# Other row lengths for the first query and key loads, turning by products with the identity, and held gelus spread over slots

## The chip, the cores and the metric

The kernel runs on one core of one Trainium2 chip. The core has TensorE (PE; its weight loads are listed as PEld), VectorE (DVE), ScalarE (ACT), GpSimd (POOL) and SyncE (SP); DMAs are issued from queues on SP, ACT and POOL and share 16 DMA engines. Matmuls write to PSUM banks, from which DVE or ACT copy the result. The metric is the device time of one execution in microseconds (us). The kernel before was run 8 times: median 1395.11 us (1392.54 to 1398.53).

## What is computed

```python
scores = scale * np.matmul(q, k.transpose(0, 1, 3, 2))          # q, k, v: (8, 8, 576, 64) fp32
thresh = np.max(scores, axis=-1, keepdims=True) - tau
scores = np.where(scores >= thresh, scores, -1000000000.0)
attn = softmax(scores)                                          # sum + 1e-9 below the line
x = attn @ v -> (4608, 512)
h = x @ w_in; g = gelu(h); out = g @ w_out                      # w_in 512x2048, w_out 2048x512
```

The weights w_in and w_out are float64 in memory. The kernel converts them to float32 on the chip.

## The kernel before

**Attention by pairs and slots.** Two heads make a pair p, 32 pairs in all, four of them (0 to 3) belonging to the first batch and called early. The 576 rows of a pair's queries are cut into four chunks of 128 and a tail of 64; one (pair, chunk) is a slot. The main loop (L823) runs over slots in an order written out by hand: slots 0 to 7 are chunks 0 and 1 of pairs 0 to 3, slots 8 to 19 are chunks 2, 3 and 4 of pairs 0 to 3, and from slot 20 (BATCH) on each pair has five slots in a row. All engines execute what the loop emits in the order in which it emits it, each engine its own part.

**One slot.** `scores` (PE, L348) multiplies a chunk of qT with kT into a "sc" tile. `softmax_head` takes the negated maximum (DVE, L360), a threshold (POOL, L361) and the exponential (ACT, L363). `weigh_v` (PE, L465, for chunks that came due) multiplies the turned p with v into a tile xT, which ACT copies into `x_blk` (L470). `softmax_tail` applies the threshold and sums (DVE, L379, L382). For early pairs `diagonal` (DVE L390, ACT L393) makes a diagonal matrix of the reciprocals, and in the next slot `turn_p_early` turns p by products with that diagonal (PE, L291); ACT copies the turned p out of PSUM (L299, L302, L309, L314). Later pairs are turned by DVE (`turn_p`, L426) and DMAs.

**Queries and keys of the early pairs.** `load_early` brings the rows of a pair's two heads side by side into a tile of 128 columns per chunk. q has row c*128+p on partition p, in pieces of 256 bytes; k has row 4p+c, read as 1 KB in one run and written in pieces of 256 bytes. SP issues them, but for k of pairs 0 (ACT) and 1 (POOL). `turn_qk_early` transposes each chunk on PE (L265, tails L273) and ACT copies the result into qT, kT and q_tail (L268 to L278). It runs for pair 0 ahead of the loop and for pair p+1 in the slot of pair p and chunk 0 (slots 0, 2, 4).

**The conversion of the weights.** 32 pieces (128x512 float64, two DMAs each, `load_piece`) are converted in steps by DVE with one step on ACT (`conversions`, L168 to L178, nominal 340, 340, 720 and 700 ns on DVE). Two pieces are loaded ahead of the loop, one in slot 0, one in slot 2, and then each finished piece calls for the next one. `convert(ns)` in each slot adds a budget and does steps until it is used up: 0 in slot 0, 3400 in slots 1 to 7, 3650 in slots 8 to 18, and everything left in slot 19.

**The MLP between slots.** `block_steps` multiplies a block of 256 tokens: 16 chunks of hidden units with four products each (L536), two chunks to a PSUM tile hT, then gelu on ACT, then layer 2 (L550) into a tile o. `fill` emits as many of these products in each slot as a goal written by hand allows; for slots 10 to 19 that is 0.42 of block 0. The gelu and the exponential use different ACT tables, so `gelus` only copies hT to SBUF (L503) while `hold` is set and puts it on a list `held`; the other finished hT wait on a list `late`. At slot 20 `gelus_held` applies the gelu to all held tiles (L509), and `table` (L522) brings the exponential's table back.

**PSUM.** The pool `ps` has four one-bank buffers with the tag "mm": the tiles tr, xT, hT and o all come from it. The scores have the tag "sc" and their own buffers.

After slot 20 the remaining blocks go on beside attention; the last ten blocks are computed by `strassen` (L670), which the diff doesn't touch.

Of the kernel before, what the change touches and what calls it, by code (L numbers as in the profile page):

```python
# [8 lines left out]
FP32 = mybir.dt.float32  # L9
# [9 lines left out]
def kernel(  # L19
# [28 lines left out]
    nc = tc.nc  # L48
    ctx.enter_context(tc.manual_schedule())

    B, H, S, D = q.shape
    d_model, d_ff = moe_w_in.shape
    P = 128
    Q = 32
    HP = H // 2
    NP = B * HP
    EARLY = HP
    NC = S // P
    MAIN = NC * P
    TAIL = S - MAIN  # L60
# [4 lines left out]
    N_DF = d_ff // P  # L65
    TOK = 256
# [119 lines left out]
    def convert(ns):  # L186

        if conv["steps"] is None:
            conv["steps"] = conversions()
        conv["debt"] += ns  # L190
        while conv["debt"] > 0:
            took = next(conv["steps"], None)
            if took is None:
                return
            conv["debt"] -= took
# [3 lines left out]
    x_blk = {}  # L199
# [27 lines left out]
    def load_early(p):  # L227
        b, hp = divmod(p, HP)
        s = st[p] = {}
        for name, src in (("q", q), ("k", k)):  # L230
            t = s[name] = ld.tile([P, NC + 1, P], FP32, tag=name, name=name)
            eng = (nc.scalar, nc.gpsimd)[p] if p < 2 and name == "k" else nc.sync
            for e in range(2):
                order = "(t p) d -> p t d" if name == "q" else "(p t) d -> p t d"
                eng.dma_start(
                    t[:, 0:NC, e * D:(e + 1) * D], src[b, 2 * hp + e, 0:MAIN, :].rearrange(order, p=P))
            eng.dma_start(
                t[0:TAIL, NC, :].rearrange("p (e d) -> p e d", e=2),
                src[b, 2 * hp:2 * hp + 2, MAIN:S, :].rearrange("e s d -> s e d"),
            )  # L240

    def load_v_early(p):
        b, hp = divmod(p, HP)
# [5 lines left out]
    def turn_qk_early(p):  # L249


        s = st[p]
        if 2 <= p < HP:
            qT = op.tile([P, MAIN], FP32, tag="o_sb", name="qT")
            kT = pd_tail[p - 2].rearrange("p b i -> p (b i)")
        else:
            qT = ld.tile([P, MAIN], FP32, tag="qT", name="qT")
            kT = ld.tile([P, TAIL + S], FP32, tag="kT", name="kT")
        s["qT"], s["kT"] = qT, kT
        qt = s["q_tail"] = q_tail[p % 4]  # L260
        for name in "qk":
            t = s[name]
            tr = ps.tile([P, NC, P], FP32, tag="mm", name="tr")
            for c in range(NC):
                nc.tensor.transpose(tr[:, c, :], t[:, c, :], ident)  # L265
            src = tr.rearrange("p c s -> p (c s)")
            if name == "q":
                nc.scalar.activation(qT, src, AF.Copy, bias=0.0, scale=q_scale)  # L268
            else:
                nc.scalar.copy(kT[:, TAIL:S], src)  # L270
        tr = ps.tile([P, NC, P], FP32, tag="mm", name="tr")
        for j, name in enumerate("qk"):
            nc.tensor.transpose(tr[:, j, 0:TAIL], s.pop(name)[0:TAIL, NC, :], ident[0:TAIL, 0:TAIL])  # L273
        nc.scalar.copy(kT[:, S:S + TAIL], tr[:, 1, 0:TAIL])
        nc.scalar.copy(kT[D:P, 0:TAIL], tr[D:P, 1, 0:TAIL])
        for e in range(2):
            rows = slice(e * D, (e + 1) * D)
            nc.scalar.activation(  # L278
                qt[rows, e * TAIL:(e + 1) * TAIL], tr[rows, 0, 0:TAIL], AF.Copy, bias=0.0, scale=q_scale[rows])

    def turn_p_early(p, i):


        s = st[p]
        if i == 0 or (p < HP and i == 2):
            s["pT"] = [one.tile([P, KR, S], FP32, tag=f"pT{e}", name=f"pT{e}") for e in range(2)]
        w, diag = s.pop(("p", i)), s.pop(("diag", i))
        n = 1 if i == NC else 2

        def turn(to, cols, e):  # L290
            nc.tensor.matmul(to, lhsT=w[:, cols], rhs=diag[:, e, :], start=True, stop=True)  # L291

        for e in range(n):
            tr = ps.tile([P, NC, P], FP32, tag="mm", name="tr")
            for c in range(NC):
                at = e * (S + TAIL) + c * P
                turn(tr[:, c, :], slice(at, at + P), e)
            if i < NC:
                nc.scalar.copy(s["pT"][e][:, 0:NC, i * P:(i + 1) * P], tr)  # L299
        if i == NC:  # L300
            for e in range(2):
                nc.scalar.copy(s["pT"][e][:, 0:NC, MAIN:S], tr[:, :, e * TAIL:(e + 1) * TAIL])  # L302
        tails = s["pT"][0][:, NC, :]
        tr = ps.tile([P, NC, P], FP32, tag="mm", name="tr")
        if i < NC:
            for e in range(2):
                at = MAIN + e * TAIL
                turn(tr[e * TAIL:(e + 1) * TAIL, 0, :], slice(at, at + TAIL), e)
            nc.scalar.copy(tails[:, i * P:(i + 1) * P], tr[:, 0, :])  # L309
            return  # L310
        turn(tr[0:TAIL, 0, :], slice(MAIN, S), 0)
        for e in range(2):
            rows = slice(e * TAIL, (e + 1) * TAIL)
            nc.scalar.copy(tails[rows, MAIN:S], tr[0:TAIL, 0, rows])  # L314

    def scale_q(p):
        t = st[p]["q"]
# [132 lines left out]
    def weigh_v(p, lo, hi):  # L450


        b, hp = divmod(p, HP)
        s = st[p]
        xT = ps.tile([P, 512], FP32, tag="mm", name="xT")
        for c in range(KR):
            for e in range(2):
                f = slice(e * D, (e + 1) * D)
                to = xT[f, 0:hi - lo]
                if p < EARLY:  # L460
                    rhs = s["pT"][0 if c == NC else e][:, c, lo:hi]
                else:
                    to = to.rearrange("p (g s) -> p g s", s=2 * Q)
                    rhs = by_64(s["pT"][e])[:, lo // (2 * Q):hi // (2 * Q), c, :]
                nc.tensor.matmul(  # L465
                    to, lhsT=s["v"][:, e, c, :], rhs=rhs, start=(c == 0), stop=(c == KR - 1))
        for n, o, at, size in in_blocks(b, lo, hi):
            if n not in x_blk:
                x_blk[n] = xg.tile([P, N_DM, TOK], FP32, tag="x", name="x")
            nc.scalar.copy(x_blk[n][:, hp, o:o + size], xT[:, at - lo:at - lo + size])  # L470

    def in_blocks(b, lo, hi):
        while lo < hi:
# [22 lines left out]
    def gelus(left):  # L496


        while len(late) > left:
            g, j, hT = late.pop(0)  # L500
            t = gp.tile([P, 2, TOK], FP32, tag="g", name="g")
            if hold[0]:
                nc.scalar.copy(t, hT)  # L503
                held.append((g, j, t))
            else:
                gelu(g, j, t, hT)
# [3 lines left out]
        g[j - 1], g[j] = t[:, 0, :], t[:, 1, :]  # L510
        dirty[0] = True

    def gelus_held():
        hold[0] = False
        while held:
            g, j, t = held.pop(0)
            gelu(g, j, t, t)

# [6 lines left out]
    def block_steps(n):  # L525

        g = {}
        mlp["layer"] = 1
        for j in range(N_DF):
            if j % 2 == 0:  # L530
                hT = None
            for c in range(N_DM):
                yield NS_IN, (j * P // PIECE + 1) * N_DM
                if hT is None:
                    hT = ps.tile([P, 2, TOK], FP32, tag="mm", name="hT")
                nc.tensor.matmul(hT[:, j % 2, :], lhsT=w_in_sb[c][:, j * P:(j + 1) * P], rhs=x_blk[n][:, c, :],  # L536
                                 start=(c == 0), stop=(c == N_DM - 1))
            if j % 2:
                late.append((g, j, hT))
                gelus(lag[0])  # L540
        for m in range(TOK // P):
            for j in range(N_DF):
                mlp["layer"] = 2
                yield NS_OUT, len(pieces) - N_DF + j + 1
                if j not in g:
                    gelus(0)
                    gelus_held()
                if j == 0:
                    o = ps.tile([P, 512], FP32, tag="mm", name="o_ps")
                nc.tensor.matmul(o[:, 0:d_model], lhsT=g[j][:, m * P:(m + 1) * P], rhs=w_out_sb[j],  # L550
                                 start=(j == 0), stop=(j == N_DF - 1))
            o_sb = op.tile([P, d_model], FP32, tag="o_sb", name="o_sb")
            nc.scalar.copy(o_sb, o[:, 0:d_model])
            row = n * TOK + m * P
            nc.sync.dma_start(out[row:row + P, :], o_sb)
# [267 lines left out]
    for n in range(len(slots) + WEIGH + 1):  # L823
# [5 lines left out]
            softmax_head(p, i)  # L829
        elif n == len(slots):  # L830
            ext = weights_in()
        gelus(0)
        if n == BATCH:
            gelus_held()
        table()
        for args in due:
            weigh_v(*args)
# [46 lines left out]
            scale_q(p + 1)  # L884
        if p >= HP - 1 and i == 2 and p + 1 < NP:
            turn_qk(p + 1)
        convert(0 if n == 0 else 3400 if n < 2 * HP else 3650 if n < BATCH - 1 else 1e9)
        if early:
            diagonal(p, i)
        if not early:  # L890
# [51 lines left out]
```

## Time and profile before

| what | value |
|---|---|
| median of 8 runs | 1395.11 us (1392.54 to 1398.53) |
| the profiled execution | 1392.52 us, span 1390.7 us |
| PE busy | 1359.2 us, 98% |
| DVE busy | 891.4 us, 64% |
| ACT busy | 640.9 us, 46% |
| POOL busy | 432.3 us, 31% |
| mean granted TensorE clock | 0.994 |
| DMA queue q1 (SP and others) | 194768 packets, 112.84 MB |
| DMA queue q0 (POOL) | 23488 packets, 54.77 MB |

The profile is of one execution. The span runs from the first instruction to the last; 1.8 us of the execution's time lie around it. "Busy" counts the time in which an engine had an instruction running, whatever bounds it. Views that are used below: the busy share in 40 slices of the span, in tenths; the chain of work that ended last; tables of busy time by stretches of time, with the granted clock (1.00 is full speed) and the DMA engines' mean share; and timelines, in which each row is a start, a duration, an engine, a line, an operation, what it writes and reads, its count, and in brackets how long the engine had stood idle and what released it. A product in fp32 has two records on PE, a transpose one.

### The profile page before, as it was taken

The page shows a single profiled execution, that of the slowest core. Times are in us where ns is not written, and L with a number is a line of the kernel's source. Part 1 is how long each engine was busy: PE and PEld are TensorE (multiplying, and loading weights), DVE is VectorE, ACT ScalarE, POOL GpSimd, SP SyncE. Part 2 cuts the span into 40 slices and gives each one's busy share as a digit, 9 for nine tenths or more (in the row PEclk, how much of TensorE's full clock was granted, in tenths as well). Part 3 has the DMA queues.
Part 4 walks back from the last instruction along what each step waited for, and adds up shares of the span by engine and source line. Part 5 has one row for each costly group of instructions (what it writes and reads, how often), then busy time and mean ns, then how long its engine had stood idle before and what let it go on. Part 6 is the DMA issues. An engine that isn't in the chain of part 4 may idle for free.

```text
span 1390.7 us, 19980 instructions
## 1 busy us (share of the span) xinstructions
PE 1359.2 (98%) x6608; PEld 967.7 (70%) x6608; DVE 891.4 (64%) x1734; ACT 640.9 (46%) x1165; POOL 432.3 (31%) x895
## 2 busy tenths in 40 slices
PE   6799899999999999999999999999999999999999
PEld 5676557557457466466466475588888888888887
DVE  5889677788888888888888888764132232241330
ACT  6666636547547457448367357241141240330420
POOL 4444254455455555554554551100000000000000
PEclk9899999999999999999999999999999999999999
DMA  9989267667777777787788776500000001001000
GB/s 264 270 296 292 56 135 166 131 158 169 168 163 177 160 187 183 156 195 178 157 201 180 158 181 132 118 0 8 23 1 23 23 1 46 16 0 53 9 8 23
DMA packets 219557, 169.18 MB, mean 122 GB/s; under 512 B 121456, under 2 KB 203952, under 8 KB 219456
## 3 DMA queue, kind: packets, MB, share of 16 engines
q1 hardware_dynamic: 194768, 112.84, 36.1%
q0 software_dynamic: 23488, 54.77, 13.3%
q8 instruction: 54, 0.88, 0.3%
q10 hardware_dynamic: 1200, 0.30, 0.1%
q14 instruction: 47, 0.39, 0.1%
HBM read 72.73 MB, written 12.52 MB: 61 GB/s over the span
## 4 chain that ended last, share of the span: by engine, by line
PE 89%; DVE 5%; ACT 3%; DMA 2%; issue 1%; SPq 1%; POOL 0%; DVEq 0%; ACTq 0%; POOLq 0%
PE bank L670 35%; PE o_ps L550 16%; PE hT L536 14%; PE sc L348 12%; PE xT L465 10%; DVE p L379 1%; ACT p L363 1%; PE tr L291 1%; DVE power L176 1%; DMA raw<-in_moe_w_out_dram 1%; ACT diag L393 1%; DVE power L168 1%; DVE w_in L178 0%; DVE nmx L360 0%; DVE w_out L178 0%
## 5 line engine op out<-in xcount | busy, mean ns | idle before, releaser
L363 ACT ACTIVATE p<-sc,nmx 128x576 f32<-128x576 f32 x288 | 201.9, 738 | 270.3 <-DVE nmx L360 270.2
L379 DVE SCALAR_TENSOR_TENSOR p<-sc,thr,p 128x576 f32<-128x576 f32 x288 | 225.4, 816 | 70.4 <-ACT p L363 67.6
L360 DVE TENSOR_REDUCE nmx<-sc 128x1 f32<-128x576 f32 x288 | 205.3, 750 | 67.4 <-PE sc L348 66.6
L536 PE MATMUL hT<-x,w_in 128*128 128x256 f32 x1024 | 241.1, 385 | 0.0
L550 PE MATMUL o_ps<-w_out,g 128*128 128x512 f32 x512 | 236.8, 603 | 2.1 <-ACT pT L302 2.1
L536 PEld LDWEIGHTS hT<-x,w_in 128*128 128x128 f32 x1024 | 189.5, 190 | 49.2 <-issue 23.5
L361 POOL TENSOR_SCALAR thr<-nmx,tau_eff 128x1 f32<-128x1 f32 x288 | 84.0, 292 | 394.5 <-DVE nmx L360 394.1
L550 PEld LDWEIGHTS o_ps<-w_out,g 128*128 128x128 f32 x512 | 92.9, 189 | 112.7 <-issue 108.6
L465 PE MATMUL xT<-pT,v 128*64 128x256 f32 (+1 forms) x1280 | 163.9, 409 | 0.5 <-issue 0.5
L348 PE MATMUL sc<-kT,qT 64*128 64x288 f32 x960 | 158.6, 433 | 3.3 <-DVE p L379 1.7
L426 DVE STREAM_TRANSPOSE turned_p<-p 128x1152 f32<-128x1152 f32 x112 | 154.4, 1378 | 3.9
L348 PEld LDWEIGHTS sc<-kT,qT 64*128 64x128 f32 x960 | 90.6, 188 | 76.8 <-issue 64.4
L465 PEld LDWEIGHTS xT<-pT,v 128*64 128x64 f32 x1280 | 89.0, 137 | 72.9 <-issue 13.3
L670 PE MATMUL bank<-x,w_in 128*128 128x256 f32 x480 | 116.7, 379 | 0.0
L670 PE MATMUL bank<-w_out,unit 128*128 128x256 f32 x520 | 115.5, 379 | 0.0
L223 POOL DMA_DIRECT2D v<-in_v_dram x208 | 110.7, 535 | 4.7 <-issue 3.1
L670 PEld LDWEIGHTS bank<-w_out,unit 128*128 128x128 f32 x520 | 98.8, 190 | 13.4
L670 PEld LDWEIGHTS bank<-x,w_in 128*128 128x128 f32 x480 | 91.2, 190 | 12.8 <-issue 0.5
L670 PE MATMUL bank<-v,unit 128*128 128x256 f32 x320 | 82.1, 379 | 0.0
L214 POOL DMA_DIRECT2D q<-in_q_dram x104 | 70.7, 685 | 10.0 <-issue 9.1
L670 PE MATMUL bank<-unit,turned_p 128*128 128x256 f32 x320 | 73.1, 379 | 0.0
L522 ACT ACT_TABLE_LOAD x56 | 71.8, 1283 | 1.0
(154 smaller groups left out, 1486.7 us busy)
## 6 DMA issues: line engine op xcount, KB each, us to landing
pT<-turned_p SPq DMA_DIRECT2D x448, 160.0 KB, 3.7
pT<-pd_tail SPq DMA_DIRECT2D x112, 80.0 KB, 3.1
q<-in_q_dram POOLq DMA_DIRECT2D x104, 72.0 KB, 3.3
k<-in_k_dram POOLq DMA_DIRECT2D x104, 72.0 KB, 3.2
inv<-turned SPq DMA_DIRECT2D x56, 128.0 KB, 4.0
v<-in_v_dram POOLq DMA_DIRECT2D x156, 40.0 KB, 3.2
x<-x SPq DMA_DIRECT2D x10, 512.0 KB, 4.6
raw<-in_moe_w_out_dram POOLq DMA_DIRECT2D x8, 512.0 KB, 5.5
```

Of the source, the lines that this page charges most:

```text
L223: eng.dma_start(t[r:P:4, e, 0:n, :], rows[:, r * KR:r * KR + n, :])
L348: nc.tensor.matmul(sc[e][:, h, 0:HALF], lhsT=lhsT, rhs=s["kT"][rows, at:at + HALF], start=True, stop=True)
L360: nc.vector.tensor_reduce(nmx[:, e:e + 1], sc, axis=AXIS.XY, op=ALU.max, negate=True)
L361: nc.gpsimd.tensor_scalar(thr[:, e:e + 1], nmx[:, e:e + 1], -1.0, tau_eff, op0=ALU.mult, op1=ALU.subtract)
L363: nc.scalar.activation(w[:, e * S:(e + 1) * S].rearrange("p (h s) -> p h s", h=2), sc, AF.Exp, bias=nmx[:, e:e + 1], scale=1.0)
L379: nc.vector.scalar_tensor_tensor(row, sc[e][:, :, 0:HALF], thr[:, e:e + 1], row, op0=ALU.is_ge, op1=ALU.mult, accum_out=den[e])
L426: nc.vector.transpose(turned_p[:, :, i // 2, 0:NB, i % 2 * Q:(i % 2 + 1) * Q], w.rearrange("p (e b i) -> p e b i", e=2, i=Q))
L465: nc.tensor.matmul(to, lhsT=s["v"][:, e, c, :], rhs=rhs, start=(c == 0), stop=(c == KR - 1))
L522: nc.scalar.activation(warm[:, 1:2], warm[:, 0:1], AF.Exp)
L536: nc.tensor.matmul(hT[:, j % 2, :], lhsT=w_in_sb[c][:, j * P:(j + 1) * P], rhs=x_blk[n][:, c, :], start=(c == 0), stop=(c == N_DM - 1))
L550: nc.tensor.matmul(o[:, 0:d_model], lhsT=g[j][:, m * P:(m + 1) * P], rhs=w_out_sb[j], start=(j == 0), stop=(j == N_DF - 1))
L670: nc.tensor.matmul(to, lhsT=l, rhs=r, start=start and k == 0, stop=k == len(pairs) - 1, skip_group_check=not start)
```

## The change

1. `load_early`: the tile becomes [128, 2 heads, 5, 64]. A partition reads two neighbouring rows of q (512 bytes, chunk pair g and row 2p+c of it) and four of k (1 KB) in one piece.
2. `turn_qk_early`: each transpose becomes two products with the identity, one per head, each into its half of the PSUM partitions (8 instead of 4 for q and for k, 4 instead of 2 for the tails).
3. `weigh_v`: q's chunks now hold even and odd rows, so that the copy of an early pair's 256-token xT into `x_blk` puts every second column in its place.
4. `turn_p_early`: for the last early pair (in slot 20) the four copies of the turned p's tail (L302, L314) are on DVE, not ACT.
5. The held gelus: from slot 20 on at most four per slot. `gelus(0)` at the head of a slot, and `gelus(lag)` inside a block once `hold` is off, run only when nothing is held. So in slots 10 to 19, once one tile is held, an hT is copied only when the next one is finished.
6. The conversion's budget is 0 in slot 0, 2000 in slots 1 and 2, 3800 in slots 3 to 18.

```diff
-            t = s[name] = ld.tile([P, NC + 1, P], FP32, tag=name, name=name)
+            t = s[name] = ld.tile([P, 2, NC + 1, D], FP32, tag=name, name=name)
             eng = (nc.scalar, nc.gpsimd)[p] if p < 2 and name == "k" else nc.sync
             for e in range(2):
-                order = "(t p) d -> p t d" if name == "q" else "(p t) d -> p t d"
-                eng.dma_start(
-                    t[:, 0:NC, e * D:(e + 1) * D], src[b, 2 * hp + e, 0:MAIN, :].rearrange(order, p=P))
...
+                rows = src[b, 2 * hp + e, 0:MAIN, :]
+                if name == "q":
+                    eng.dma_start(t[:, e, 0:NC, :].rearrange("p (g c) d -> p g (c d)", c=2),
+                                  rows.rearrange("(g p c) d -> p g (c d)", p=P, c=2))
+                else:
+                    eng.dma_start(t[:, e, 0:NC, :], rows.rearrange("(p t) d -> p t d", p=P))
...
             for c in range(NC):
-                nc.tensor.transpose(tr[:, c, :], t[:, c, :], ident)
+                for e in range(2):
+                    nc.tensor.matmul(tr[e * D:(e + 1) * D, c, :], lhsT=t[:, e, c, :], rhs=ident, start=True, stop=True)
...
-            nc.tensor.transpose(tr[:, j, 0:TAIL], s.pop(name)[0:TAIL, NC, :], ident[0:TAIL, 0:TAIL])
+            t = s.pop(name)
+            for e in range(2):
+                nc.tensor.matmul(tr[e * D:(e + 1) * D, j, 0:TAIL], lhsT=t[0:TAIL, e, NC, :],
+                                 rhs=ident[0:TAIL, 0:TAIL], start=True, stop=True)
...
         if i == NC:
+            copy = nc.vector.tensor_copy if p == EARLY - 1 else nc.scalar.copy
             for e in range(2):
-                nc.scalar.copy(s["pT"][e][:, 0:NC, MAIN:S], tr[:, :, e * TAIL:(e + 1) * TAIL])
+                copy(s["pT"][e][:, 0:NC, MAIN:S], tr[:, :, e * TAIL:(e + 1) * TAIL])
...
-            nc.scalar.copy(x_blk[n][:, hp, o:o + size], xT[:, at - lo:at - lo + size])
+            to, x = x_blk[n][:, hp, o:o + size], xT[:, at - lo:at - lo + size]
+            if p < EARLY and size == TOK:
+                to = to.rearrange("q (p c) -> q c p", c=2)
+                x = x.rearrange("q (c p) -> q c p", c=2)
+            nc.scalar.copy(to, x)
...
-    def gelus_held():
-        hold[0] = False
-        while held:
+    def gelus_held(n):
+        for _ in range(min(n, len(held))):
             g, j, t = held.pop(0)
             gelu(g, j, t, t)
...
                 late.append((g, j, hT))
-                gelus(lag[0])
+                if hold[0] or not held:
+                    gelus(lag[0])
...
                 if j not in g:
+                    gelus_held(N_DF)
                     gelus(0)
-                    gelus_held()
...
-        gelus(0)
-        if n == BATCH:
-            gelus_held()
+        if n >= BATCH:
+            hold[0] = False
+            gelus_held(4)
+        if not held:
+            gelus(0)
         table()
...
-        convert(0 if n == 0 else 3400 if n < 2 * HP else 3650 if n < BATCH - 1 else 1e9)
+        convert(0 if n == 0 else 2000 if n < 3 else 3800 if n < BATCH - 1 else 1e9)
```

More of the change, by code (lines that the diff above doesn't have):

```diff
@@ L230, in load_early @@
         for name, src in (("q", q), ("k", k)):
-            t = s[name] = ld.tile([P, NC + 1, P], FP32, tag=name, name=name)
+            t = s[name] = ld.tile([P, 2, NC + 1, D], FP32, tag=name, name=name)
             eng = (nc.scalar, nc.gpsimd)[p] if p < 2 and name == "k" else nc.sync
             for e in range(2):
-                order = "(t p) d -> p t d" if name == "q" else "(p t) d -> p t d"
-                eng.dma_start(
-                    t[:, 0:NC, e * D:(e + 1) * D], src[b, 2 * hp + e, 0:MAIN, :].rearrange(order, p=P))
[L237 to L240, printed above, removed]
+                rows = src[b, 2 * hp + e, 0:MAIN, :]
[4 more added lines that the diff above has]
+                    eng.dma_start(t[:, e, 0:NC, :], rows.rearrange("(p t) d -> p t d", p=P))
+            eng.dma_start(t[0:TAIL, :, NC, :], src[b, 2 * hp:2 * hp + 2, MAIN:S, :].rearrange("e s d -> s e d"))
     def load_v_early(p):
@@ L313, in turn_p_early @@
             rows = slice(e * TAIL, (e + 1) * TAIL)
-            nc.scalar.copy(tails[rows, MAIN:S], tr[0:TAIL, 0, rows])
+            copy(tails[rows, MAIN:S], tr[0:TAIL, 0, rows])
     def scale_q(p):
```

## The prediction, as put on record before the change was run

> **What bounds the kernel now.** I read the page first (busy shares in 40 slices, chain that ended last), then the table by stretches of 20 us, then waits and timelines of DVE, PE, ACT and SP up to 175 us, where every edit lies.
>
> ```profile
> PE   6799899999999999999999999999999999999999
> ...
> DVE  5889677788888888888888888764132232241330
> ...
> PE 89%; DVE 5%; ACT 3%; DMA 2%; issue 1%; SPq 1%; POOL 0%; DVEq 0%; ACTq 0%; POOLq 0%
> ```
>
> ```profile
> 20.00:40.00 20.00, 13.76 (x86) 10.67 (x86) 14.95 (x33) 12.38 (x27) 7.99 (x16) 0.83 0.98 306
> ...
> 120.00:140.00 20.00, 18.42 (x111) 13.65 (x110) 17.54 (x40) 12.82 (x27) 7.27 (x17) 1.00 0.92 289
> 140.00:160.00 20.00, 17.00 (x101) 12.68 (x101) 12.09 (x25) 14.33 (x28) 2.56 (x11) 1.00 0.01 1
> ...
> 180.00:200.00 20.00, 20.00 (x94) 9.47 (x94) 15.85 (x29) 6.31 (x13) 9.01 (x18) 1.00 0.65 144
> ```
>
> Columns: stretch, length, busy PE, PEld, DVE, ACT, POOL, granted clock, DMA share, GB/s. There are two regimes. Up to slot 20 (about 148 us) DVE is full but for waits: softmax plus conversion of 32 weight pieces, 2.0 us each (52.49 to 54.49). Summing its waits from the first maximum (10.63) to that of slot 20 (148.17) gives 17.5 us. From 160 us PE is full to the end, and its work there is not changed. So the change is worth two numbers: how much earlier slot 20 begins, and what PE loses in slots 20 and 21.
>
> **Loads.** From 1 to 4 us the queue of these loads moved 1056 packets, 0.26 MB, for 38.6% of 16 engines: 18.5 us, 68 ns per KB. From 10 to 14 us, with large packets, it took 61.9 us for 1.33 MB, 46.5 ns per KB. A pair moves 512 KB: (68 - 46.5) x 512 / 16 = 0.7 us; four pairs 2.8 us of DMA time, an estimate from these rows. It counts only where something waits for DMA; I take 0.3 us at the start. Order and number of DMAs on SP, ACT and POOL stay.
>
> **Turning.** Eight transposes and two tails take 26.30 to 27.37, 1.07 us. In their place stand 16 products and four tails. L465, whose products alternate halves of the array likewise, runs ten 256-column products in 2.38 us, so 0.11 us for 128 columns: 16 x 0.11 + 0.2 = 2.0 us. Ends: 1.1 (as now) and 3.9 (L291's 0.23 us per product, no overlap). I take 2.0, its row being nearest: +0.95 per pair on PE. Slot 0 ran at half speed (four transposes 1.09 us, later 0.60): products end near 8.4 instead of 7.0, kT is copied, scores begin near 8.8 instead of 8.31. But PE is then busy 4 us without a break, so the scores may take 1.2 us to the first maximum instead of 2.3: 10.0 against 10.63. Ends 9.7 and 11.1.
>
> **Conversion budgets.** These lines carry it (start, duration, engine, line, operation, idle before and its releaser):
>
> ```profile
> 22.45 3.92 PE L291 MATMUL tr<-diag,p 128*128 128x128 f32 x20 [3.08 <-ACT diag L393]
> ...
> 55.19 2.42 PE L291 MATMUL tr<-diag,p 128*128 128x128 f32 x20 [2.60 <-ACT diag L393]
> ```
>
> ```profile
> 26.92 0.69 DVE L178 SCALAR_TENSOR_TENSOR w_in<-w_in,power 128x512 f32<-128x512 uint32 x1
> 31.51 0.43 DVE L168 TENSOR_SCALAR power<-raw 128x512 uint32<-128x512 uint32 x1 [3.90 <-DMA raw<-in_moe_w_in_dram]
> ```
>
> With 3400 in slots 1 and 2 DVE reaches piece 4 (issued on POOL at 26.05) before it has landed and stands 3.9 us, softmax of slot 3 queued behind. With 2000 it does piece 0 in slot 1 and piece 1 in slot 2. Slot 1: conversion 17.35 to 19.9, so slot 2's maximum at 19.97 instead of 21.82. Slot 2: softmax 3.3, conversion 2.0, DVE free at 25.2. What is late next is slot 3's scores: p's turn on PE from 20.6 (3.9 us if the clock is halved after 2 us of idleness, as at 22.45), the new products 2.0, scores 1.1: 27.6 against 31.93. ACT then still copies qT and kT and makes the diagonal before slot 3's exponentials (29.2), 1.05 us more. Carried on with these durations, slot 6 begins 4.4 us earlier (bounds: 6 if no half clock falls in slots 2 and 4; 1.5 if the products don't overlap).
>
> The conversions put off are paid back: 400 more per slot in 6 and 7, 150 in each of 8 to 18, 850 less in 19; at 0.95 ns of DVE per unit (2.0 us for 2100) 0.76 + 1.57 - 0.80 = 1.5 us. **Slot 20 begins 4.4 - 1.5 = 2.9 us earlier.** That cover is thin: from 81 to 148 us PE is busy 65.2 of 67 us as well.
>
> **Held gelus.** Slots 20 and 21 now:
>
> ```profile
> 150.25 4.58 PE L536 MATMUL hT<-x,w_in 128*128 128x256 f32 x20
> 150.36 1.28 ACT L509 ACT_TABLE_LOAD   x1
> ...
> 151.39 1.38 DVE L426 STREAM_TRANSPOSE turned_p<-p 128x1152 f32<-128x1152 f32 x1
> 151.66 3.23 ACT L509 ACTIVATE g<-g 128x512 f32<-128x512 f32 x6
> ...
> 156.97 1.13 PE L550 MATMUL o_ps<-w_out,g 128*128 128x512 f32 x2 [2.14 <-ACT pT L302]
> ...
> 159.20 2.91 PE L465 MATMUL xT<-pT,v 128*64 128x320 f32 x20
> ...
> 160.09 1.41 ACT L363 ACTIVATE p<-sc,nmx 128x576 f32<-128x576 f32 x2 [2.86 <-DVE nmx L360]
> ...
> 161.52 1.28 ACT L509 ACT_TABLE_LOAD   x1
> ...
> 162.81 1.08 ACT L509 ACTIVATE g<-hT 128x512 f32<-128x512 f32 x2
> ```
>
> Records come two to a product, so slot 20 has ten L536 products and one L550. Layer 1's 64 products are 54 done by slot 19; eight make a pair. Tag "mm" has four banks. Now a finished hT is copied away at the next slot's head, so that hT pairs 6 and 7, o and one free bank stand at slot 21, and xT starts at once. After the change a finished hT is copied only when the next is finished (lag 1, once anything is held): at slot 20 pairs 0 to 4 are held and **pair 5 still sits in its bank**. Four held gelus leave one, so neither the slot's head nor layer 1 releases a bank, and pairs 5, 6, 7 and o take all four.
>
> Slot 20: pair 7 needs the bank of p's tail, which DVE now frees after L426: 152.77 + 2 x 0.33 = 153.5 (DVE's copy isn't in the trace; ACT's 128x256 copies come 0.32 apart, DVE's 128x576 maximum takes 0.75, so 0.6 to 1.5; I take the low end, the copy being the same). PE ends pair 6 at 151.1, waits 2.4, does eight products (3.4) and L550 by 157.8: as now. The 2.14 us that moving the copies off ACT removes comes back as a wait for the bank. Slot 21: xT now waits until ACT has done two exponentials (to 161.5), a table load (162.8), the fifth held gelu and pair 5's (0.54 each): 163.95 instead of 159.20, **+4.75 us**. Behind xT on PE stand L550 and slot 22's scores, and behind these DVE and ACT.
>
> PE idles 5 us there. Rows: idle 3.08 us before 22.45 was followed by half clock and 3.92 us for what took 2.42 at 55.19; idle 2.14 before 156.97 by none. So the restart costs 0 to 2 us (half of 4); I take 1.7, plus 0.4 for the chance that slot 20's 2.4 us does it too.
>
> [...]
>
> **Edits at nothing.** The permuted x copies (eight, 0.37 us each on ACT; at double price 3 us, spread over slots in which ACT is busy 44 of 67 us). The number of table loads is the same: two in slot 20, two in 21. Should four DVE copies in slot 20 cost 1.9 us, pair 7 starts 0.8 later.
>
> **Sum**, on the profiled execution (1392.52 us, span 1390.7 and 1.8 around it): -2.9 + 4.75 + 1.7 + 0.4 = +3.95, 1396.5, 0.28% more. The runs shown have a median of 1395.11, 2.6 above that execution; the same share gives 1399.0.
>
> **Rivals.** (1) *Same*: the early gain is near its upper end (no half clock in slots 2 and 4, 1.5 + 3 more: 4.5 to 6) and the stall costs little clock: -5 + 4.75 + 0.8 = +0.5, 1395.7. For: at 55.19 PE kept full clock after 2.60 us. Against: four of the five early gaps (3.08, 2.00, 1.84, 2.71 us; not that of 2.60) halved it. 0.24. (2) *Faster*: xT finds a bank (fewer hT waiting than I count, or o not begun in slot 20). Then the 2.14 goes for good: -2.9 - 2.1 = -5.0, 1390.1; it decides as soon as one bank is free at slot 21's head. Against: the count of 54 rests on the rows. 0.22. (3) *No early gain*: the products run alone and slots 2 to 4 wait for them (3 x 1.9): G is 0, +6.9, 1402. Part of the slower cases. (4) The loads don't get faster at all: 0.3 us, inside the forecast.
>
> **How the numbers follow.** Forecast 0.40, rival 3 0.14, together slower 0.54; same 0.24; faster 0.22. A measurement of this kernel can tell about 0.2% (2.8 us) from no change. Range 1390.2 to 1402.5, reaching from rival 2 to rival 3.
>
> **What would show it.** Right: no DMA wait of DVE near 27 us; slot 20's scores 2 to 4 us earlier; in slot 21 L465 waits about 4.7 us for ACT's gelu of hT, with the clock at half after it; L302 on DVE. Wrong: L465 starts with slot 21's scores; slot 20 more than 5 us earlier, or not earlier.

## The result and the profile after

The changed kernel takes **1400.5 us** (median of 11 runs, 1396.5 to 1402.58) beside 1395.03 us for the kernel before (31 runs, 1391.84 to 1398.53): ratio 1.0036, interval 1.0027 to 1.0045. It is slower by some 5 us. The profiled execution took 1402.58 us (span 1400.8), the longest of its runs, while that of the kernel before (1392.52, span 1390.7) is among the shortest of its own. So the two traces lie 10.1 us apart, twice the difference of the medians. What the traces explain are those 10.1 us.

First the end of the story, to know where to look. Slot 22's first maximum comes at 167.80 us before and at 177.72 after; from there to the end of the span it takes 1222.9 and 1223.1 us. So what sets these two executions apart happens before 178 us. The rows of DVE for slots 3, 20 and 22 before, and for slots 20 and 22 after:

```profile
31.93 1.40 DVE L360 TENSOR_REDUCE nmx<-sc 128x1 f32<-128x576 f32 x2
...
148.17 1.40 DVE L360 TENSOR_REDUCE nmx<-sc 128x1 f32<-128x576 f32 x2
...
167.80 1.42 DVE L360 TENSOR_REDUCE nmx<-sc 128x1 f32<-128x576 f32 x2 [3.89 <-PE sc L348]
```

```profile
148.79 1.42 DVE L365 TENSOR_REDUCE nmx<-sc 128x1 f32<-128x576 f32 x2
...
177.72 1.42 DVE L365 TENSOR_REDUCE nmx<-sc 128x1 f32<-128x576 f32 x2 [11.46 <-PE sc L353]
```

The table by stretches of 20 us of the changed kernel (columns as above: length, busy PE, PEld, DVE, ACT, POOL, granted clock, DMA share, GB/s):

```profile
20.00:40.00 20.00, 17.11 (x168) 14.20 (x168) 15.97 (x37) 15.04 (x32) 7.66 (x16) 0.91 0.92 297
...
120.00:140.00 20.00, 16.59 (x99) 12.20 (x98) 17.33 (x38) 10.22 (x23) 6.40 (x14) 0.95 0.74 271
140.00:160.00 20.00, 17.14 (x87) 13.34 (x86) 11.32 (x24) 12.01 (x21) 1.98 (x10) 0.88 0.00 1
160.00:180.00 20.00, 14.03 (x50) 5.78 (x48) 6.43 (x10) 8.83 (x14) 4.04 (x9) 0.83 0.37 81
```

and its last stretch in the kernel before:

```profile
160.00:180.00 20.00, 18.40 (x64) 8.42 (x61) 14.65 (x26) 9.75 (x15) 10.15 (x21) 1.00 0.46 103
```

From 20 to 40 us PE is busy 3.35 us longer than before and the clock is better (0.91 against 0.83): a part of it is the products, but the early slots do run ahead. From 120 us on the clock, 1.00 before in each of these stretches, is 0.95, 0.88 and 0.83, and from 160 to 180 us PE stands for 6 of 20 us where it stood for 1.6.

The early part, in the timelines of PE and DVE of the changed kernel (start, duration, engine, line, operation, idle before and its releaser):

```profile
21.00 3.61 PE L295 MATMUL tr<-diag,p 128*128 128x128 f32 x20 [1.82 <-ACT diag L398]
...
38.29 1.04 PE L266 MATMUL tr<-ident,q 128*64 128x128 f32 x16
...
40.52 1.24 PE L353 MATMUL sc<-pd_tail,qT 64*128 64x288 f32 x8
```

```profile
28.35 1.42 DVE L365 TENSOR_REDUCE nmx<-sc 128x1 f32<-128x576 f32 x2 [2.71 <-PE sc L353]
```

The first PE row, a turn of p behind a stop of 1.82 us, comes up again at the end. The second begins a pair's products with the identity and the third is what follows them: 38.29 to 40.52, 2.23 us for a pair. DVE's wait for a DMA near 27 us (3.90 us before) is gone; slot 3's maximum now waits for the scores and comes 3.58 us earlier (28.35, was 31.93).

Slots 20 and 21, the timelines of PE and ACT of the changed kernel:

```profile
150.73 1.13 PE L544 MATMUL hT<-x,w_in 128*128 128x256 f32 x4
154.21 5.38 PE L544 MATMUL hT<-x,w_in 128*128 128x256 f32 x16 [2.35 <-DVE pT L307]
159.42 1.02 PE L559 MATMUL o_ps<-w_out,g 128*128 128x512 f32 x2
160.38 1.24 PE L353 MATMUL sc<-kT,qT 64*128 64x288 f32 x8
166.32 5.60 PE L470 MATMUL xT<-pT,v 128*64 128x320 f32 x20 [4.71 <-ACT g L518]
```

```profile
162.44 1.41 ACT L368 ACTIVATE p<-sc,nmx 128x576 f32<-128x576 f32 x2 [6.44 <-DVE nmx L365]
163.86 1.28 ACT L518 ACT_TABLE_LOAD   x1
165.16 0.63 ACT L518 ACTIVATE g<-g 128x512 f32<-128x512 f32 x1
165.69 1.55 ACT L518 ACTIVATE g<-hT 128x512 f32<-128x512 f32 x3
```

Read the bracket of the last PE row: the array stood 4.71 us for a gelu. A product doesn't need a gelu of hT to compute xT; it needs the *bank* that this hT occupies (e7 below tests this). ACT shows why it takes so long: two exponentials, a table load, one gelu of a tile held in SBUF (g<-g), and only then the first gelu that reads PSUM (g<-hT). And both waits are followed by half clock (granted 0.50 from 156 to 158 and from 166 to 172 us): 16 records in 5.38 us where 20 took 4.58 before, and xT in 5.60 us, 2.91 before.

### The profile page after: what moved, and what is told of

The parts are those of the page before. It is cut to its first block, busy times and chain, and to the rows that moved or that the text cites. A ratio compares the mean times of both kernels' runs of the same rounds, so it can differ in the third digit from the quotient of the medians.

```text
span 1400.8 us, 20213 instructions
## 1 busy us (share of the span) xinstructions
PE 1365.8 (98%) x6728; PEld 971.7 (69%) x6728; DVE 893.1 (64%) x1738; ACT 639.7 (46%) x1160; POOL 432.9 (31%) x895
## 4 chain that ended last, share of the span: by engine, by line
PE 90%; DVE 4%; ACT 2%; DMA 2%; issue 1%; SPq 1%; POOL 0%; DVEq 0%; POOLq 0%; ACTq 0%
PE bank L679 35%; PE o_ps L559 16%; PE hT L544 15%; PE sc L353 12%; PE xT L470 10%; DVE p L384 1%; PE tr L295 1%; ACT p L368 1%; DVE power L176 1%; DMA v<-in_v_dram 1%; PE tr L266 1%; DMA turned_p<-in_moe_w_in_dram 1%; ACT diag L398 0%; DVE w_in L178 0%; DMA k<-in_k_dram 0%
## 5 line engine op out<-in xcount | busy, mean ns | idle before, releaser
L353 PE MATMUL sc<-kT,qT 64*128 64x288 f32 x960 | 155.7, 429 | 2.3 <-DVE p L384 1.9
```

Of the source, the lines that this page charges most:

```text
L353: nc.tensor.matmul(sc[e][:, h, 0:HALF], lhsT=lhsT, rhs=s["kT"][rows, at:at + HALF], start=True, stop=True)
```

## The experiments

The theory was: **banks**. A finished hT that is copied only when the next one is finished keeps a bank of tag "mm" into slots 20 and 21, so that xT waits there, and the clock falls behind the wait; the other parts gain or cost nothing. The rival was that the **early part** (loads, products, budgets) costs and the waits of slots 20 and 21 only take up what is there anyway. All kernels compute the whole result. For each, the first maximum on DVE of some slots, in us of its own profile:

| kernel | ratio to the kernel before [interval] | slot 3 | slot 20 | slot 22 | span |
|---|---|---|---|---|---|
| before | | 31.93 | 148.17 | 167.80 | 1390.7 |
| after | 1.0036 [1.0027, 1.0045] | 28.35 | 148.79 | 177.72 | 1400.8 |
| e1, heads emptied up to slot 19 | 0.9945 [0.9930, 0.9960] | 28.05 | 145.95 | 163.03 | 1384.6 |
| e2, gelus as before | 0.9950 [0.9935, 0.9966] | 29.62 | 148.77 | 165.85 | 1388.8 |
| e3, gelus alone | 1.0087 [1.0071, 1.0103] | 31.22 | 148.61 | 179.80 | 1406.2 |
| e4, loads and products alone | 0.9996 [0.9983, 1.0008] | 30.91 | 147.12 | 166.75 | 1388.2 |
| e5, budgets alone | 0.9979 [0.9965, 0.9993] | 26.53 | 146.42 | 166.08 | 1391.4 |
| e6, DVE copies alone | 0.9968 [0.9955, 0.9981] | 31.52 | 149.09 | 166.32 | 1389.2 |
| e7, after, layer 2 not before slot 21 | 0.9988 [0.9977, 0.9999] | 26.49 | 145.94 | 169.23 | 1392.5 |
| e8, products alone | 1.0005 [0.9994, 1.0016] | 32.68 | 150.38 | 171.61 | 1392.8 |
| e9, budgets and DVE copies | 0.9941 [0.9925, 0.9957] | 27.71 | 145.64 | 162.74 | 1388.2 |
| e10, e9 and four gelus, heads emptied | 0.9950 [0.9931, 0.9970] | 26.15 | 144.60 | 161.69 | 1384.6 |

The slots' times are those of one execution each and scatter: in e8 slot 22 comes 3.8 us later than before, at a ratio of 1.0005. What an edit is worth is read from the ratio, where it goes from the rows.

### e1: the changed kernel with the banks emptied

One line: up to slot 19 the head of a slot copies every finished hT to SBUF, as before the change.

```diff
-        if not held:
+        if n < BATCH or not held:
             gelus(0)
```

> The changed kernel, but up to slot 19 the head of each slot copies every finished hT away, as in the kernel before; from slot 20 on the gelus stay four per slot. Theory (banks): pairs 0 to 5 are then held at slot 20, only 6 and 7 keep a bank, so xT of slot 21 starts right behind the scores, without the 4.7 us wait for ACT and without the half clock after it: 5 to 7 us less than the changed kernel, 0.998 to 1.000 of the kernel before. Rival (the early part: products, loads or budgets cost the time): the wait doesn't matter or comes back elsewhere, 1.003.

Measured: 1386.6 us beside 1394.51, ratio 0.9945. That is 0.91%, or 12.7 us, below the changed kernel, where 5 to 7 us were expected. The PE timeline of this kernel, slots 20 and 21:

```profile
147.88 4.58 PE L544 MATMUL hT<-x,w_in 128*128 128x256 f32 x20
152.30 1.02 PE L559 MATMUL o_ps<-w_out,g 128*128 128x512 f32 x2
153.25 1.24 PE L353 MATMUL sc<-kT,qT 64*128 64x288 f32 x8
154.42 2.91 PE L470 MATMUL xT<-pT,v 128*64 128x320 f32 x20
```

No brackets and full clock (granted 1.00 from 140 to 180 us): ten hT products in one stretch, o, scores and xT behind one another. From slot 20 to slot 22 this takes 17.08 us, 28.93 in the changed kernel: the waits (2.35 + 4.71) and the half clock after them (5.60 - 2.91 = 2.69 for xT; for the 16 hT records 5.38 - 3.72 = 1.66, since 4 records take 1.13 and 20 take 4.58, 0.216 for each more) make 11.41 of these 11.85 us. The four gelus per slot are still there, so it is the late copy and not their number. The theory of the banks holds; and with them free the change gains 0.55%.

### e2 and e3: the gelus taken out, and alone

e2 is the changed kernel with the old handling of the gelus; e3 is the kernel before with the new one (the same lines, turned round):

```diff
-    def gelus_held():
-        hold[0] = False
-        while held:
+    def gelus_held(n):
+        for _ in range(min(n, len(held))):
...
-                gelus(lag[0])
+                if hold[0] or not held:
+                    gelus(lag[0])
...
-        gelus(0)
-        if n == BATCH:
-            gelus_held()
+        if n >= BATCH:
+            hold[0] = False
+            gelus_held(4)
+        if not held:
+            gelus(0)
```

> The changed kernel with the whole handling of held gelus as before (all six at slot 20, every head copies). Loads, products, budgets and the copies on DVE stay. Theory (banks): no wait of xT, layer 2's first product no longer waits for ACT's copies (2.1 us): 0.997 to 1.000 of before, within 1.5 us of the run that only frees the heads. Rival (early part): 1.003.

> The kernel before with the four-per-slot gelus alone; the copies of the last tail stay on ACT. Theory (banks): xT of slot 21 waits 4 to 5 us for ACT, and pair 7 waits longer than in the changed kernel, since its bank is freed by ACT behind four gelus and a table load: 1.004 to 1.008. Rival (early part): 0.999 to 1.001.

Measured: 0.9950 without the new gelus and 1.0087 with nothing else; both lie on the side expected and a little beyond the bounds given. The PE timeline of e3, in which the tail copies are still on ACT:

```profile
156.40 6.68 PE L535 MATMUL hT<-x,w_in 128*128 128x256 f32 x16 [4.59 <-ACT pT L302]
...
169.81 4.30 PE L465 MATMUL xT<-pT,v 128*64 128x320 f32 x20 [4.71 <-ACT g L509]
```

The same two waits. The first is 4.59 us, not 2.35, because ACT reaches the copy of p's tail (which frees the bank) only after four gelus and two table loads (2.19 us and 1.28 us each). The second is 4.71 us again, and the work on ACT in it is the same (exponentials 1.40 us, load 1.28, gelus 0.63 and 1.55; 1.41, 1.28, 0.63 and 1.55 in the changed kernel). The rival is out: without any of the early parts the waits are there and the kernel is 0.9% slower; with all of them and without the waits it is 0.5% faster.

### e4, e5, e6 and e8: the other parts one by one

e4 has items 1 to 3 of the change (loads, products, permuted copy of x) alone; e8 has the products on the old tiles, so that loads and products come apart. e5 and e6 are one edit each:

```diff
-        convert(0 if n == 0 else 3400 if n < 2 * HP else 3650 if n < BATCH - 1 else 1e9)
+        convert(0 if n == 0 else 2000 if n < 3 else 3800 if n < BATCH - 1 else 1e9)
```

```diff
+            copy = nc.vector.tensor_copy if p == EARLY - 1 else nc.scalar.copy
             for e in range(2):
-                nc.scalar.copy(s["pT"][e][:, 0:NC, MAIN:S], tr[:, :, e * TAIL:(e + 1) * TAIL])
+                copy(s["pT"][e][:, 0:NC, MAIN:S], tr[:, :, e * TAIL:(e + 1) * TAIL])
...
-            nc.scalar.copy(tails[rows, MAIN:S], tr[0:TAIL, 0, rows])
+            copy(tails[rows, MAIN:S], tr[0:TAIL, 0, rows])
```

and e8 is

```diff
-                nc.tensor.transpose(tr[:, c, :], t[:, c, :], ident)
+                for e in range(2):
+                    nc.tensor.matmul(tr[e * D:(e + 1) * D, c, :], lhsT=t[:, c, e * D:(e + 1) * D], rhs=ident, start=True, stop=True)
```

(and the tails likewise).

> The kernel before with the new rows of q and k, the products with the identity and the permuted copy of x alone. Theory (banks): the products hide beside DVE, 0.999 to 1.001. Rival (early part): these make the loss, 1.003.

> The kernel before with the new conversion budgets alone (2000 in slots 1 and 2, then 3800). Theory: DVE's 3.9 us wait for piece 4 goes, 1.5 us are paid back, slot 20 begins 1 to 2.5 us earlier: 0.998 to 0.9995. Rival (what is put off meets other waits, ACT's step of the conversion and the DMAs of the last pieces, in slots 16 to 19): 1.000 to 1.002, slot 20 not earlier.

> The kernel before with the four copies of the last tail on DVE alone. Theory: the wait of layer 2's first product for ACT's copies (2.1 us) goes, and with all hT copied at the heads there is no wait for a bank in its place: 0.998 to 0.9995, L550 of slot 20 right behind L536. Rival (PE then waits for the gelu or the scores are late anyway): 1.000.

> The kernel before, loads as before, but each transpose of the first pairs' q and k replaced by two products with the identity. Theory: 1 us or less more PE time per pair, most of it beside DVE, 1.000 to 1.001. Rival (the products delay the scores of slots 3 and 5, and these DVE, all the way): 1.002 to 1.003.

Measured: loads with products 0.9996 and products alone 1.0005, neither to be told from no change; budgets 0.9979; DVE copies 0.9968, the last more than expected. In the PE timeline of e6 the wait of 2.14 us ahead of layer 2 is gone:

```profile
151.17 4.58 PE L537 MATMUL hT<-x,w_in 128*128 128x256 f32 x20
155.59 1.02 PE L551 MATMUL o_ps<-w_out,g 128*128 128x512 f32 x2
```

From slot 20's maximum to slot 21's it is 8.72 us, before 11.13: 2.4 us from four copies of together 1.15 us (L307 0.72 and L319 0.43 in the changed kernel's DVE timeline, below), because on ACT they stood behind six gelus and two table loads (3.23 us and 1.28 us each before). The interval of the ratio says 2.7 to 6.3 us; what lies beyond the 2.4 isn't in this trace.

```profile
153.34 0.72 DVE L307 COPY pT<-tr 128x256 f32<-128x256 f32 x2
153.98 0.43 DVE L319 COPY pT<-tr 64x64 f32<-64x64 f32 x2
```

### e7: the changed kernel with one bank less in demand

Layer 2 of the block isn't begun before slot 21, so that o takes no bank in slot 20.

```diff
+    wait2 = [True]
...
-            if mlp["debt"] <= 0 or need > converted[0]:
+            if mlp["debt"] <= 0 or need > converted[0] or wait2[0] and need > len(pieces) - N_DF:
...
+        if n == BATCH:
+            wait2[0] = False
```

> The changed kernel, but layer 2 isn't begun before slot 21, so that o takes no bank in slot 20 (its one product moves to slot 21). Theory (banks): one bank is free at the head of slot 21, xT starts behind the scores: 3 to 6 us less than the changed kernel, 0.999 to 1.001. Rival (xT waits for something else on ACT): the wait of 4.7 us stays, 1.003.

Measured: 0.9988, just below the 0.999 to 1.001 expected. Its PE timeline:

```profile
151.35 5.38 PE L544 MATMUL hT<-x,w_in 128*128 128x256 f32 x16 [2.34 <-DVE pT L307]
156.66 1.24 PE L353 MATMUL sc<-kT,qT 64*128 64x288 f32 x8
157.83 2.91 PE L470 MATMUL xT<-pT,v 128*64 128x320 f32 x20
162.61 5.42 PE L559 MATMUL o_ps<-w_out,g 128*128 128x512 f32 x12 [1.87 <-ACT g L518]
```

With one bank more xT starts right behind the scores, so the 4.71 us were a wait for a bank and nothing else. What ACT is late with shows up one step later: layer 2 waits 1.87 us for the same gelu. That too is a wait for a bank: its first product reads the gelu of pair 0, which ACT did in slot 20, and hT pairs 5 to 7 and xT take the four banks. The wait ahead of pair 7 stays (2.34 us), and the 16 records behind it take 5.38 us again. One bank freed brings 0.48% of the changed kernel's time back (1.0036 to 0.9988), all of them (e1) 0.91%.

### e9 and e10: only what gains

e9 is the kernel before with the edits of e5 and e6; e10 adds to it the four gelus per slot with emptied heads (e3's lines and e1's).

> The kernel before with two of the five parts of the change: the conversion budgets and the four tail copies on DVE. Theory (the early parts gain, the late gelus cost, loads and products are worth nothing): the two ratios measured alone add up, 0.9979 and 0.9968 give 0.9947; 1387.5 to 1388.5 us beside a median of 1395.0. If the loads with the products help only where the budgets make use of them, this stays above the version that had both (0.9950 with before's gelus): 0.998 or more. Slot 20 at about 146 us, slot 21 at 154 to 157 us.

> The same and the gelus made four per slot, but with finished hT tiles copied at every slot's head up to slot 19, so that no bank is held into slots 20 and 21. Old loads, transposes. Theory (four gelus per slot are harmless when the banks are free): within 0.1% of the run beside it, 0.9945 as in the version with the new loads. If four per slot has a price of its own (the four held tiles that are left for slot 21 delay its exponentials or gelus), it is 0.3% or more above the run beside it. xT of slot 21 starts right behind the scores, no wait for ACT's gelu of hT.

Measured: 1388.55 us beside 1396.72 for e9, ratio 0.9941, where the two alone give 0.9947; and 0.9950 for e10, not to be told from e9. So loads, products and four gelus per slot are worth nothing that these runs can tell from zero in any combination tried, and two edits of some lines beat both kernels by 0.6% (before) and, through their ratios, 0.95% (after). The PE timeline of e9 has slot 21's xT behind its scores:

```profile
152.97 1.24 PE L349 MATMUL sc<-kT,qT 64*128 64x288 f32 x8
154.14 2.91 PE L466 MATMUL xT<-pT,v 128*64 128x320 f32 x20
```

## Why the prediction was right, and where its terms were off

The median came at 1400.5 where 1399.0 was forecast, in the range, on the side forecast, and by the mechanism forecast. In the profiled executions the sum was +3.95 and the difference is +10.1. Term by term:

| step | forecast | measured in the profiles |
|---|---|---|
| slot 20 begins earlier | -2.9 | +0.6 (148.79 against 148.17) |
| wait ahead of pair 7, in place of the 2.14 | +0.3 | +0.2 (2.35) |
| clock after it | +0.4 (as a chance) | +1.66 |
| xT's wait in slot 21 | +4.75 | +4.71 |
| clock after it | +1.7 | +2.69 |
| sum | +3.95 (the second line not counted in it) | +9.9; slot 22 is 9.9 later |

- **Held gelus**: the count of banks was right, and both waits within 0.05 us: pair 7 waits for DVE's copy (2.4 forecast), xT for two exponentials, a table load (1.28 us), one held gelu and one from PSUM (4.75). The wait of 2.14 us that the copies on DVE remove does come back as a wait for the bank, as the step said; e6 and e1 show that it goes for good where banks are free. The late copies also cost before slot 20: in slot 17 of the changed kernel a tr waits 0.57 us for ACT's copy of a g, which e1's timeline doesn't have (scores 3.20 us behind the slot's maximum, 2.77 in e1).
- **Conversion budgets**: slot 6 begins 4.1 us earlier (54.56 to 50.46; forecast 4.4) and the wait for the piece near 27 us is gone. Over all runs what the payback leaves of it is about the size forecast too: alone (e5) the budgets are worth 2.9 us by the ratio (1.0 to 4.9), and slot 20 comes 1.75 us earlier in e5, 2.2 in e1 and e7, 2.5 in e9 and 3.6 in e10 (forecast 2.9). In the profiled execution of the changed kernel nothing of it is left, nor in that of e2, where slot 20 comes 0.6 us later as well. Slot 16 of the changed kernel begins at 118.48, 1.54 us after e1's. About 1.1 of these were lost over slots 5 and 6, where DVE waits 0.52 and 0.53 us for a piece's DMA, which it doesn't in e1; in slot 18 the turn then runs at half clock and loses 1.56 more (3.98 us, 2.42 in e7). In e2 the turn in slot 4 took 3.96 us, 2.42 in the changed kernel. So the step left out what differs from one execution to the next.
- **Loads and turning**: 2.23 us for a pair's products against 2.0 forecast, 1.07 before. The first maximum comes at 10.46, 10.0 forecast, 1.28 us behind the start of its scores (9.18; 1.2 set, 2.32 before); the products ended at 8.9 (8.4 forecast). A gain of 0.3 us was set on the loads; e4 and e8 bound it to nothing that a median shows.
- **Clock**: set at 2.1 us for both waits, measured 4.35, and 1.56 in slot 18. This is a mis-sized term: "0.4 for the chance" was a mean over two outcomes, of which one came, and the 2.69 us behind xT's wait lie outside the 0 to 2 us given as bounds, within which the 1.7 was the author's estimate.
- **Rivals**: (2), that xT finds a bank, is what e1 makes true: slot 22 then comes 4.8 us earlier than before the change, where the rival's sum was 5.0 (by the ratio 7.7). Its condition, a free bank at slot 21's head, is what decides. (3) is out by the 3.58 us that slot 3 gains. (1) had its clock term far too low.

**How much of the match is luck.** The ratios split the change in two. With the banks emptied (e1) it gains 0.55%, 7.7 us (5.6 to 9.8), where rival (2), the same case, had 5.0. The late copies then cost 0.91%, 12.7 us, where the prediction has 8.95, from -5.0 to +3.95. Both sizes were about a third too small, with opposite signs, and what is left of them, 5.0 against 3.95, agrees better than either. In the gain it is the copies on DVE that were too small: 0.32%, 4.5 us (e6), for the 2.14 us of their wait. The mechanism is shown; the closeness of the sum is in part luck.

**Why the medians differ by 5 us and the profiled executions by 10.1.** The three stretches at half clock make 5.9 us of the profiled difference, and each execution on record has its mean granted clock. The two profiled ones have 0.994 (before) and 0.990 (after); the fastest of the changed kernel, 1396.5 us, has 0.994 too. In the 60 executions of the kernel before that were run beside e1, e5 and e9 those at 0.990 took 1399.2 us in the mean (two of them) and those at 0.995 1392.1, about 1.4 us for each 0.001. So the clock alone sets the profiled pair some 5.6 us apart, an estimate from these rows. **What stays open** is which stretches ran at half clock in executions without a trace, and what the copies on DVE gain beyond 2.4 us.

## What to carry to other kernels

Work put off on one engine holds whatever storage its input sits in: before a copy out of PSUM is made lazy, count for each later slot which tiles of the same pool are then alive, the waiting ones too, and who frees the next. In these profiles a wait for a buffer is named by the instruction that frees it, so "a product waits for a gelu that it doesn't read" was here the sign of one buffer too few: 4.71 us ahead of xT, put down to L518, and none in e7 with one bank more. And take a bundle of edits apart: here two of six carried the whole gain and one more than undid it.

## What the runs showed of the hardware

The clock after a short stop of PE differs from one execution to the next. The turn of p in slot 6, 20 records, in the PE timelines of e1 and of e2 (the same early work, the same wait):

```profile
50.38 2.42 PE L295 MATMUL tr<-diag,p 128*128 128x128 f32 x20 [2.71 <-ACT diag L398]
```

```profile
53.47 3.75 PE L295 MATMUL tr<-diag,p 128*128 128x128 f32 x20 [2.71 <-ACT diag L398]
```

Equal waits of 2.71 us, full clock in one execution (granted 1.00 from 40 to 60 us, 2.42 us for the turn), less in the other (0.90 over the same 20 us, 3.75 us for it). The wait of 2.17 us for a bank in slot 18 likewise: half clock in the changed kernel (granted 0.50 from 138 to 140 us), full in e7 (1.00 from 120 to 140 us):

```profile
138.08 3.98 PE L295 MATMUL tr<-diag,p 128*128 128x128 f32 x20 [2.17 <-ACT x L479]
```

```profile
136.78 2.42 PE L295 MATMUL tr<-diag,p 128*128 128x128 f32 x20 [2.17 <-ACT x L479]
```

A wait of 1.82 us early in slot 2 was followed by slower turns in e1, e2, e9 and the changed kernel (3.59, 3.31, 3.46 and 3.61 us; in the last the granted clock is 0.50 from 22 to 25 us). In e5 and e10, with the same early work as e9, slot 3's maximum comes 5.40 us behind slot 2's, 6.95 in e9; in e7, with that of e1, 6.38, 7.98 in e1. So one profile can't price a stop of 1.8 to 2.7 us; on the turn behind it the price was 0 or, in these rows, 0.9 to 1.6 us, and the sum should keep both.

In the changed kernel stops of 1.82, 2.17 and 2.35 us were followed by a granted clock of 0.50 (from 22 to 25, 138 to 140 and 156 to 158 us), and one of 1.89 us by 1.00 (from 36 to 39 us, 2.42 us for the turn). What decides it, no run here shows.
